# Two more pairs of tiles by seven products, the quarter sums of w_out in earlier slots, and batch 2 a slot sooner

## The chip, the core and the metric

One core of a Trainium2 chip runs the whole kernel. The metric is the device time of one execution in microseconds (us); where several executions are shown, it is their median. A profile is one execution, recorded by the hardware profiler. The engines are named as the profile names them: PE (matmul), PEld (PE's weight load), DVE (vector), ACT (scalar), POOL (GpSimd) and SP (sync, which only issues DMAs here).

## What is computed

Attention with a sliding window and a linear bias, then a two-layer network with ELU. q, k and v have 8 batches, 8 heads, 576 positions and a head size of 64; w_in is 512 x 2048, w_out 2048 x 512; everything is float32 in DRAM.

```
scores = q @ k.T / 8 ;  rel = i - j
scores = scores - slope[h] * |rel|   where 0 <= rel < 128, else -1e9
x = softmax(scores) @ v              # to 4608 tokens x 512 (batch, position; head, d)
h = x @ w_in
g = h if h > 0 else exp(h) - 1
out = g @ w_out                      # 4608 x 512
```

## The kernel before

All inputs are turned to float16 as they are loaded; sums are float32 in PSUM. The 4608 tokens are 9 blocks t of 512 (NTB = 9) for the second part, and 8 batches of 576 for the attention, so attention runs a little ahead of the blocks that use it.

**Slots.** The program's order is written out by hand (`tc.manual_schedule()`): each engine works through its instructions in the order in which the program gives them. A loop at the end (L655 on) goes through numbered slots s. In each slot it gives, in this order: the `early` entries; the hidden step of the slot (`HID`, one [128 x 512] PSUM bank of h: 16 or so matmuls of L305); `done(s-1)`, the DVE half of ELU for the slot before; the `tasks` (attention steps, turns, loads, sums); the output work of the slot (`OUT`); and the `late` entries. `at_once` puts an entry at the head of the tasks, `before` and `after` into `early` and `late`. Slots 0 to 17 hold the hidden steps of block 0 and two of block 1; slots 18 to 23 have no hidden step, as the first batch's positions are used up; from slot 24 on every slot has one. Slot 11 starts at about 34 us, slot 18 at 48.3, slot 24 at 57.2, slot 31 at 69.8, slot 38 at 84.6, slot 48 at 104.5.

**Hidden and ELU.** `hidden` (L297) computes h into one of two or three PSUM banks in turn (`BUF`), and ELU is max(min(exp(h), 1) - 1, h). In a plain slot ACT takes exp (L315), POOL clamps (L316); in a slot of the set `SOFT` ACT does both, as exp(-relu(-h)) in two instructions (L312, L313), and POOL does nothing. DVE then subtracts 1 and takes the maximum with the PSUM bank (L323, `elu`), into g, in the slot after. `e`, between ACT, POOL and DVE, is a ring of six tiles.

**Output.** A pair n is 256 tokens (two row tiles of 128; block t has pairs 2t and 2t+1). A pair is multiplied with w_out in one of two ways. The plain way (`output`, L327) takes 4 matmuls of 512 columns per slot, 32 for a pair; a tile's sum lies in one PSUM bank, is copied by ACT (`store`, L336) and sent by SP. The other way (Strassen's, in Winograd's form) takes the halves of the pair's rows, of the 2048 and of the 512, and needs seven products of quarter size (`product`, L387) instead of eight: 7 x 8 matmuls of 256 columns, seven matmuls to a slot over eight slots. For it DVE makes four sums of g per pair (`sums`, L363, 128 x 1024 float16 each), ACT keeps copies of four partial results (`kept`, L396) and copies one (L398), and DVE makes three combines (`combine`, L400: C11, C12, C22, 128 x 256 float32). Four sums of quarters of w_out, T[1] to T[4], are made once, by DVE, in eight halves (`quarters`, L356). The products of a pair accumulate in two PSUM banks, `XY[n]`: products 1, 6, 7 and 4 in the first, 2, 5 and 3 in the second; 6 has to wait until ACT has copied 1, 5 until C11 has read 2, and so on. `SEVEN` is the set of pairs done so.

**Attention.** From batch 2 on, `START[b]` is the slot in which a batch begins; unit u (128 keys against 256 queries) begins 4 slots after the one before. `scores` (L218) fills four banks (spa, sp[2], sp[3]), ACT takes exp in the next two slots (`expo`, L233 and L236), DVE multiplies with the bias table (`weigh`, L241), and three slots after the scores `all_values` (L263) multiplies with v into spa; DVE divides into `xn` (L277, L260), a ring of six tiles, and `turn` (L280) transposes it into xT, by DMA on SP from batch 2 on and on PE with a copy by ACT before. The last 64 rows of a batch (`values`, unit 4) use sp[2] and sp[3], one slot after unit 3. Batches 0 and 1 are done in smaller steps (`turn_first`, `first_scores`, `first_weigh`, `values`), batch 1 in slots 16 to 32, its q and k turned on PE (L136, copies L140).

The eight PSUM banks are spa (two), sp[2], sp[3], hp[0], hp[1], av and op.

Of the kernel before, what the change touches and what calls it, by code (L numbers as in the profile page):

```python
# [18 lines left out]
def kernel(  # L19
# [35 lines left out]
    RB = one([128, 512], F16, "RB")  # L55

    SI = one([128, H, 128], F16, "SI")
# [28 lines left out]

    T = [None] + [s1[:, 2048 * i:2048 * i + 2048].rearrange("p (j c) -> p j c", j=8) for i in range(3)]
    T.append(one([128, 8, 256], F16, "T4"))

# [59 lines left out]
    with tc.manual_schedule():  # L149
# [93 lines left out]
        def values(b, i, part, bank=av):  # L243

            m = 128 if i < 4 else 64
            banks = (part, part + 2) if b < 2 else (2 * part, 2 * part + 1)
            parts = [(3, 128, 3), (3, 192, 4)] if i == 4 else [(i, 0, i)] + ([(i - 1, 128, i - 1)] if i else [])
            a = bank[:, 0:4 * (D + 1)].rearrange("p (x h d) -> p x h d", x=2, h=2)
            for x, g in enumerate(banks):
                for h2 in range(2):  # L250
                    for j, (u, c, n) in enumerate(parts):
                        c += 512 * g + 256 * h2
                        nc.tensor.matmul(a[:, x, h2, :], ex_[u][:, c:c + 128], VP[b % 2][:, n, 2 * g + h2, 0:D + 1],  # L253
                                         start=j == 0, stop=j == len(parts) - 1)
            if part == 0:
                xnt[b, i] = work.tile([128, 4, 2, D], F16, name="xn", tag="xn", bufs=6)
            o = xnt[b, i][0:m, part::2, :, :] if b < 2 else xnt[b, i][0:m, 2 * part:2 * part + 2, :, :]
            r = work.tile([128, 2, 2], F32, name="rden", tag="rden", bufs=2)
            V.reciprocal(out=r[0:m], in_=a[0:m, :, :, D])
            V.tensor_tensor(out=o, in0=a[0:m, :, :, 0:D], in1=r[0:m].unsqueeze(3).broadcast_to([m, 2, 2, D]),  # L260
                            op=ALU.mult)

        def all_values(b, i):  # L263
# [9 lines left out]
            xnt[b, i] = work.tile([128, 4, 2, D], F16, name="xn", tag="xn", bufs=6)  # L273
# [23 lines left out]
        def hidden(t, c0, w, f0, nf, p, soft):  # L297
# [10 lines left out]
            e = es[t, c0, f0] = work.tile([128, 512], F32, name="e", tag="e", bufs=6)  # L308
# [111 lines left out]
        wz = one([128, 256], F16, "wz")  # L420
# [7 lines left out]
        rel = one([128, 256], I32, "rel")  # L428
        far = one([128, 256], F16, "far")
# [89 lines left out]
        SEVEN = range(3, 18)  # L519

        XY = {1: (op, av)}
        for n in range(2, 2 * NTB):
            XY[n] = XY[n - 1][::-1] if n - 1 in SEVEN else XY[n - 1]
        for o in range(16 * NTB):
# [4 lines left out]
            OUT[s] = [(output, (t, ts, 4 * f, (op, op, sp[3], op)[ts] if t == 0 else XY[o // 8 or 1][ts % 2]))]  # L529
# [52 lines left out]
        for u, a0, a1, d in ((0, 18, 19, 2), (1, 20, 21, 2), (2, 22, 24, 0), (3, 26, 28, 0)):  # L582
# [5 lines left out]
            at(a1 + 3, turn, 1, u, nc.scalar.copy, (op, av, sp[3], sp[3])[u])  # L588
        at(24, turn_first, 1, 1, 1, 0, sp[3], nc.scalar.copy)
# [5 lines left out]
        START = [None, None, 32, 48, 66, 83, 100, 117]  # L595
# [32 lines left out]
        for m, a in enumerate((26, 30, 31, 32, 34, 35, 36, 39)):  # L628
            at_once(a, quarters, 1 + m // 2, m % 2)
        turns = [(i, j) for i in (1, 2, 6, 5, 7, 3, 4) for j in range(8)]  # L630
        for n in SEVEN:
            s = 15 + 8 * n
            if n < 2 * NTB - 1:
                for d, i in ((-1, 1), (1, 2), (3, 3), (4, 4)):
                    at_once(s + d, sums, n, i)
                after(s + 2, combine, n, "C11")
                after(s + 6, combine, n, "C12")
                at_once(s + 8, combine, n, "C22")
                for d in range(8):
                    OUT[s + d] = [(product, (n, i, j, j + 1)) for i, j in turns[7 * d:7 * d + 7]]  # L640
# [10 lines left out]

        SOFT = {15 + 8 * n + d for n in SEVEN for d in (0, 1, 2, 3, 4, 7)} | {26, 30, 31, 32, 34, 35, 36, 39} | set(range(16 * NTB - 10, 16 * NTB + 8))

# [44 lines left out]
```

## Time and profile before

| | |
|---|---|
| Median of 5 runs | 313.14 us (312.75 to 313.47) |
| The profiled execution's own time | 312.75 us |
| Its span in the profile | 311.0 us |
| Busy: PE, weight loads | 301.9 us (97%), 251.6 us |
| Busy: DVE, ACT, POOL | 251.8 (81%), 238.0 (77%), 111.1 (36%) |
| L305 (hidden), PE | 1488 matmuls of L305 into hp, 144.3 us |
| L329 (plain output), PE | 96 matmuls in all |
| Granted PE clock | full speed in all slices |

The profile was recorded on one execution, whose own time lies 1.75 us over its span. A row of the view by stretches gives a window's start and end, its length, then for each engine the busy time and, in brackets, the number of instructions. A row of the timeline gives start and duration in us, engine and line, operation, what is written and what is read, the shapes and how many such instructions in a row; in square brackets stands the idle time before it and what ended it. A row of the chain of waits gives start, duration and line. Durations of neighbours on one engine may overlap a little, as engines take the next instruction before the last one's result is out; the distance from start to start is what an instruction holds its engine.

### The profile page before, as it was taken

What the parts mean: (1) busy time and instruction counts of PE and PEld (TensorE: products, weight loads), DVE (VectorE), ACT (ScalarE), POOL (GpSimd) and SP (SyncE); (2) the same over time, 40 slices, a digit from 0 to 9 for tenths busy, and PEclk for the clock granted to TensorE, in tenths of its full rate; (3) what the DMA queues carried; (4) which work ended last, traced back from release to release, by engine and by line L of the source; (5) the groups of instructions that cost most, each with busy time, mean ns of one, the idle gap of its engine ahead of it and who ended that gap; (6) DMA issues with size and microseconds to landing.
All of it is one profiled execution on the core that took longest, in us unless ns stands there. A gap on an engine that the chain in (4) does not pass through costs nothing.

```text
span 311.0 us, 9691 instructions
## 1 busy us (share of the span) xinstructions
PE 301.9 (97%) x4023; PEld 251.6 (81%) x4023; DVE 251.8 (81%) x484; ACT 238.0 (77%) x434; POOL 111.1 (36%) x169
## 2 busy tenths in 40 slices
PE   8799999999999999999999999999999999999995
PEld 6588774787678788988888888888899888888884
DVE  5646656789899999898989989989998788886783
ACT  5467448688878698888797889788888797968871
POOL 8748789462262316150707070806000101010000
PEclk9999999999999999999999999999999999999999
DMA  9999999987797919698999999999632312030103
GB/s 97 178 196 201 202 173 148 164 85 98 86 119 82 165 18 143 64 131 86 81 119 99 148 89 92 119 137 95 81 94 11 93 19 86 19 93 4 67 25 112
DMA packets 96508, 32.02 MB, mean 103 GB/s; under 512 B 83920, under 2 KB 91984, under 8 KB 96464
## 3 DMA queue, kind: packets, MB, share of 16 engines
q0 software_dynamic: 75920, 18.36, 66.0%
q1 hardware_dynamic: 20400, 12.98, 18.1%
q8 instruction: 31, 0.51, 0.7%
q14 instruction: 13, 0.11, 0.1%
q10 hardware_dynamic: 144, 0.07, 0.1%
HBM read 36.70 MB, written 9.44 MB: 148 GB/s over the span
## 4 chain that ended last, share of the span: by engine, by line
PE 80%; DVE 6%; DMA 4%; ACT 4%; POOL 4%; issue 2%; POOLq 0%; ACTq 0%
PE hp L305 35%; PE op L393 12%; PE av L393 12%; PE op L329 4%; PE spa L225 4%; DMA s<-in_q_dram 4%; PE spa L271 3%; DVE g L323 3%; POOL e L316 2%; ACT e L315 2%; PE sp L393 1%; PE sp L329 1%; PE sp L305 1%; PE sp L253 1%; PE av L329 1%
## 5 line engine op out<-in xcount | busy, mean ns | idle before, releaser
L305 PE MATMUL hp<-xT,wi 128*128 128x256 f16 (+3 forms) x1488 | 144.3, 245 | 1.8 <-DMA wi<-in_moe_w_in_dram 0.9
L305 PEld LDWEIGHTS <-wi 128*128 128x128 f16 x1600 | 119.4, 98 | 21.3 <-issue 6.7
L323 DVE SCALAR_TENSOR_TENSOR g<-e,hp 128x512 f16<-128x512 f32 x138 | 93.6, 679 | 26.7 <-POOL e L316 13.4
L316 POOL TENSOR_SCALAR e<-e 128x512 f32<-128x512 f32 x50 | 31.2, 625 | 159.8 <-ACT e L315 159.3
L312 ACT ACTIVATE e<-hp 128x512 f32<-128x512 f32 x94 | 56.3, 599 | 26.1 <-PE hp L305 22.2
L313 ACT ACTIVATE e<-e 128x512 f32<-128x512 f32 x94 | 59.4, 632 | 3.0
L393 PEld LDWEIGHTS <-S 128*128 128x128 f16 x480 | 45.6, 98 | 5.0
L315 ACT ACTIVATE e<-hp 128x512 f32<-128x512 f32 x44 | 26.5, 603 | 15.7 <-PE hp L305 14.4
L241 DVE TENSOR_TENSOR EX<-EX,TAB 128x1024 f16<-128x1024 f16 x48 | 33.4, 695 | 6.3 <-ACT EX L233 3.4
L393 PEld LDWEIGHTS <-g 128*128 128x128 f16 x360 | 33.9, 98 | 3.6
L114 POOL DMA_DIRECT2D VP<-in_v_dram x40 | 34.3, 866 | 2.3 <-DMA s<-in_q_dram 1.3
L233 ACT ACTIVATE EX<-spa 128x1024 f16<-128x1024 f32 x24 | 24.7, 1027 | 5.6 <-PE spa L225 5.3
L236 ACT ACTIVATE EX<-sp 128x512 f16<-128x512 f32 x48 | 26.0, 598 | 0.0
L393 PE MATMUL op<-s,S 128*128 128x256 f16 x168 | 25.2, 273 | 0.0
L393 PE MATMUL av<-s,S 128*128 128x256 f16 x168 | 25.2, 273 | 0.0
L354 DVE TENSOR_TENSOR S<-g 128x1024 f16<-128x1024 f16 (+2 forms) x31 | 20.8, 671 | 0.8 <-PE av L393 0.2
L277 DVE TENSOR_TENSOR xn<-spa,rden 128x512 f16<-128x512 f32 x24 | 16.6, 691 | 0.8
L393 PE MATMUL av<-wo,g 128*128 128x256 f16 x112 | 16.8, 272 | 0.0
L393 PE MATMUL op<-wo,g 128*128 128x256 f16 x112 | 16.8, 272 | 0.0
L329 PE MATMUL op<-wo,g 128*128 128x512 f16 x64 | 16.5, 379 | 0.0
L108 POOL DMA_DIRECT2D st<-in_k_dram x24 | 16.2, 682 | 0.1
L225 PE MATMUL sp<-QT,KT 32*128 32x256 f16 (+2 forms) x240 | 15.4, 250 | 0.7 <-DVE xn L260 0.7
(142 smaller groups left out, 388.3 us busy)
## 6 DMA issues: line engine op xcount, KB each, us to landing
out_dram<-ob SPq DMA_DIRECT2D x35, 256.0 KB, 2.6
VP<-in_v_dram POOLq DMA_DIRECT2D x32, 128.0 KB, 5.8
st<-in_k_dram POOLq DMA_DIRECT2D x24, 144.0 KB, 4.2
st<-in_q_dram POOLq DMA_DIRECT2D x24, 144.0 KB, 6.0
wi<-in_moe_w_in_dram POOLq DMA_DIRECT2D x4, 512.0 KB, 13.3
wo<-in_moe_w_out_dram POOLq DMA_DIRECT2D x4, 512.0 KB, 11.2
VP<-in_v_dram POOLq DMA_DIRECT2D x8, 64.0 KB, 5.9
s<-in_k_dram POOLq DMA_DIRECT2D x1, 512.0 KB, 13.1
```

The source lines that it names most:

```text
L114: nc.gpsimd.dma_start(VP[b % 2][0:p, n, :, 0:D], v[b, :, 128 * n:128 * n + p, :].rearrange("h p d -> p h d"))
L225: nc.tensor.matmul(sp[g][:, 256 * h2 + o:256 * h2 + o + n], kt_[b % 2][r, k0:k0 + 255:2], qt_[b % 2][r, c0:c0 + 2 * n - 1:2], start=dh == ...
L236: nc.scalar.activation(unit(b, u)[:, g, :, :], sp[g].rearrange("p (h c) -> p h c", h=2), AF.Exp, scale=0.125)
L241: V.tensor_tensor(out=e, in0=e, in1=TAB[:, int(u == 3), 2 * gp:2 * gp + 2, :, :], op=ALU.mult)
L305: nc.tensor.matmul(p[:, l * w + u0:l * w + u1], w_in_sb[:, c, fc * 128:(fc + 1) * 128], xT[:, c, x0:x0 + u1 - u0], start=(c == 0), stop=(c ...
L312: nc.scalar.activation(e[:, 0:n], p[:, 0:n], AF.Relu, scale=-1.0)
L313: nc.scalar.activation(e[:, 0:n], e[:, 0:n], AF.Exp, scale=-1.0)
L315: nc.scalar.activation(e[:, 0:n], p[:, 0:n], AF.Exp)
L316: nc.gpsimd.tensor_scalar(out=e[:, 0:n], in0=e[:, 0:n], scalar1=1.0, scalar2=0.0, op0=ALU.min, op1=ALU.max)
L323: V.scalar_tensor_tensor(out=gs[t][:, f0:f0 + nf, c0:c0 + w], in0=sh(es.pop((t, c0, f0))), scalar=1.0, in1=sh(hps.pop((t, c0, f0))), op0=A ...
L329: nc.tensor.matmul(o, gs[t][:, fc, ts * 128:(ts + 1) * 128], w_out_sb[:, fc, :], start=(fc == 0), stop=(fc == NFC - 1))
L393: nc.tensor.matmul(o, a[:, j, :], b[:, j, :], start=j == 0 and i in (1, 2, 5), stop=j == 7, skip_group_check=True)
```

## The change

- `SEVEN` grows from pairs 3 to 17 to pairs 1 to 17. Pair 0 alone stays plain. Pair 1 takes the slots that its plain form had, 19 to 23, 25, 27 and 29 (`ps`); pair 2 takes 31 to 38. The number of slots with output work is the same.
- The eight halves of T[1] to T[4] go from slots 26, 30 to 32, 34 to 36 and 39 to slots 11 to 18.
- T[1] to T[3] lay in `s1`, the staging tile of batch 1's q and k; they get tiles of their own. The room comes from `RB`, `SI`, `wz`, `rel` and `far`, small tables of the start, which now lie in those tiles, and from the rings of xn and e, four deep in place of six.
- `SOFT` becomes: slots 11 to 18, slots of pairs 2 to 17 by the old rule, and 20, 22 and 23 (which have no hidden step). So 11 to 17, 33 and 38 become soft, and 26, 30 and 36 plain.
- `START[2]` goes from 32 to 31: all of batch 2's attention is a slot sooner, and the loads for batch 3, which are placed by it, too. Batch 3 stays at 48.
- Banks: pair 1 uses op and sp[3]; from pair 2 on the two banks alternate; the turns of batch 1's units 0 and 2 use av, and the last turn of its k goes from slot 24 and sp[3] to slot 25 and av.

```diff
--- before.py
+++ after.py
@@ -52,9 +52,12 @@
     ident = one([128, 128], F16, "ident")
 
 
-    RB = one([128, 512], F16, "RB")
-
-    SI = one([128, H, 128], F16, "SI")
+
+    T = [None] + [one([128, 8, 256], F16, f"T{i}") for i in (1, 2, 3, 4)]
+    fore = [t.rearrange("p j c -> p (j c)") if t is not None else None for t in T]
+    RB = fore[3][:, 1024:1536]
+
+    SI = fore[3][:, 0:1024].rearrange("p (h c) -> p h c", h=H)
 
     TAB = one([128, 2, 4, 2, 256], F16, "TAB")
 
@@ -83,9 +86,6 @@
     s0 = gpool.tile([128, NFC * 512], F16, name="s0", tag="g")
     s1 = one([128, 2 * H * 6 * D], F16, "s1")
     s0 = [t[:, 0:2 * H * 6 * D].rearrange("p (w h j d) -> p w h j d", w=2, h=H, j=6) for t in (s0, s1)]
-
-    T = [None] + [s1[:, 2048 * i:2048 * i + 2048].rearrange("p (j c) -> p j c", j=8) for i in range(3)]
-    T.append(one([128, 8, 256], F16, "T4"))
 
     def split(b, w, part):
 
@@ -253,7 +253,7 @@
                         nc.tensor.matmul(a[:, x, h2, :], ex_[u][:, c:c + 128], VP[b % 2][:, n, 2 * g + h2, 0:D + 1],
                                          start=j == 0, stop=j == len(parts) - 1)
             if part == 0:
-                xnt[b, i] = work.tile([128, 4, 2, D], F16, name="xn", tag="xn", bufs=6)
+                xnt[b, i] = work.tile([128, 4, 2, D], F16, name="xn", tag="xn", bufs=4)
             o = xnt[b, i][0:m, part::2, :, :] if b < 2 else xnt[b, i][0:m, 2 * part:2 * part + 2, :, :]
             r = work.tile([128, 2, 2], F32, name="rden", tag="rden", bufs=2)
             V.reciprocal(out=r[0:m], in_=a[0:m, :, :, D])
@@ -270,7 +270,7 @@
                     c += 256 * h
                     nc.tensor.matmul(a[:, h // 4, h % 4, :], ex_[u][:, c:c + 128], VP[b % 2][:, n, h, 0:D + 1],
                                      start=j == 0, stop=j == len(parts) - 1)
-            xnt[b, i] = work.tile([128, 4, 2, D], F16, name="xn", tag="xn", bufs=6)
+            xnt[b, i] = work.tile([128, 4, 2, D], F16, name="xn", tag="xn", bufs=4)
             o = xnt[b, i][0:m].rearrange("p (t g) h d -> p t (g h) d", t=2)
             r = work.tile([128, 2, 4], F32, name="rden", tag="rden8", bufs=2)
             V.reciprocal(out=r[0:m], in_=a[0:m, :, :, D])
@@ -305,7 +305,7 @@
                         nc.tensor.matmul(
                             p[:, l * w + u0:l * w + u1], w_in_sb[:, c, fc * 128:(fc + 1) * 128],
                             xT[:, c, x0:x0 + u1 - u0], start=(c == 0), stop=(c == 3))
-            e = es[t, c0, f0] = work.tile([128, 512], F32, name="e", tag="e", bufs=6)
+            e = es[t, c0, f0] = work.tile([128, 512], F32, name="e", tag="e", bufs=4)
             n = w * nf
             if soft:
 
@@ -417,7 +417,7 @@
                 copy(tile_out(n, 1)[:, c0:c0 + 128], o[:, c0:c0 + 128])
                 put(n, 1, c0, c0 + 128, queue)
 
-        wz = one([128, 256], F16, "wz")
+        wz = fore[4][:, 0:256]
 
         def warm(n, bank=op):
             for _ in range(n):
@@ -425,8 +425,8 @@
 
 
 
-        rel = one([128, 256], I32, "rel")
-        far = one([128, 256], F16, "far")
+        rel = fore[3][:, 1536:2048].bitcast(I32)
+        far = fore[1][:, 0:256]
         V.memset(wz, 1.0)
         load_first(0, 1, 0)
         nc.gpsimd.iota(rel, pattern=[[1, 256]], base=0, channel_multiplier=-1)
@@ -516,17 +516,17 @@
             for j in range(16):
                 step = (256 * (j // 8), 256, 2 * (j % 8), 2)
                 HID[16 * t + 6 + j] = [(t, *step, BUF[(j + 1) % 2])]
-        SEVEN = range(3, 18)
-
-        XY = {1: (op, av)}
-        for n in range(2, 2 * NTB):
-            XY[n] = XY[n - 1][::-1] if n - 1 in SEVEN else XY[n - 1]
+        SEVEN = range(1, 18)
+
+        XY = {1: (op, sp[3]), 2: (op, av)}
+        for n in range(3, 2 * NTB):
+            XY[n] = XY[n - 1][::-1]
         for o in range(16 * NTB):
             t, ts, f = o // 16, o // 4 % 4, o % 4
             if o // 8 in SEVEN:
                 continue
             s = (9, 11, 13, 14)[o] if o < 4 else 11 + o if o < 13 else 2 * o - 1 if o < 16 else 15 + o
-            OUT[s] = [(output, (t, ts, 4 * f, (op, op, sp[3], op)[ts] if t == 0 else XY[o // 8 or 1][ts % 2]))]
+            OUT[s] = [(output, (t, ts, 4 * f, op))]
 
         def done(r):
             for step in HID[r]:
@@ -585,14 +585,14 @@
                 at(a, first_expo, 1, u, half, d * half, 0, 256)
                 at(a + 1, first_weigh, 1, u, half)
                 at(a + 2, values, 1, u, half, av if half else sp[2])
-            at(a1 + 3, turn, 1, u, nc.scalar.copy, (op, av, sp[3], sp[3])[u])
-        at(24, turn_first, 1, 1, 1, 0, sp[3], nc.scalar.copy)
+            at(a1 + 3, turn, 1, u, nc.scalar.copy, (av, av, av, sp[3])[u])
+        at(25, turn_first, 1, 1, 1, 0, av, nc.scalar.copy)
         at(30, values, 1, 4, 0, sp[2])
         at(31, values, 1, 4, 1)
         at(32, turn, 1, 4)
 
 
-        START = [None, None, 32, 48, 66, 83, 100, 117]
+        START = [None, None, 31, 48, 66, 83, 100, 117]
 
         TURN = [None, None, (22, 24, 25, 28), (40, 42, 44, 46)]
         REST = 32, 33, 36, 37
@@ -625,19 +625,20 @@
                 at(a + 3 + n if a else 20 + n // 2, load_v, b, n)
 
 
-        for m, a in enumerate((26, 30, 31, 32, 34, 35, 36, 39)):
+        for m, a in enumerate(range(11, 19)):
             at_once(a, quarters, 1 + m // 2, m % 2)
         turns = [(i, j) for i in (1, 2, 6, 5, 7, 3, 4) for j in range(8)]
         for n in SEVEN:
             s = 15 + 8 * n
+            ps = (19, 20, 21, 22, 23, 25, 27, 29, 30) if n == 1 else range(s, s + 9)
             if n < 2 * NTB - 1:
                 for d, i in ((-1, 1), (1, 2), (3, 3), (4, 4)):
-                    at_once(s + d, sums, n, i)
-                after(s + 2, combine, n, "C11")
-                after(s + 6, combine, n, "C12")
-                at_once(s + 8, combine, n, "C22")
+                    at_once(ps[d] if d > 0 else ps[0] - 1, sums, n, i)
+                after(ps[2], combine, n, "C11")
+                after(ps[6], combine, n, "C12")
+                at_once(ps[8], combine, n, "C22")
                 for d in range(8):
-                    OUT[s + d] = [(product, (n, i, j, j + 1)) for i, j in turns[7 * d:7 * d + 7]]
+                    OUT[ps[d]] = [(product, (n, i, j, j + 1)) for i, j in turns[7 * d:7 * d + 7]]
             else:
                 at_once(s - 3, sums, n, 3)
                 for i in (2, 1):
@@ -649,7 +650,7 @@
                               (product, (n, 4)), (last_out, (n,))]
 
 
-        SOFT = {15 + 8 * n + d for n in SEVEN for d in (0, 1, 2, 3, 4, 7)} | {26, 30, 31, 32, 34, 35, 36, 39} | set(range(16 * NTB - 10, 16 * NTB + 8))
+        SOFT = {15 + 8 * n + d for n in SEVEN[1:] for d in (0, 1, 2, 3, 4, 7)} | set(range(11, 19)) | {20, 22, 23} | set(range(16 * NTB - 10, 16 * NTB + 8))
 
         slots = set(HID) | set(OUT) | set(tasks) | set(early)
         for s in range(min(slots), max(slots) + 1):
```

## The prediction

> **What bounds the kernel now.** I read three views. First the busy time of each engine by stretch, cut at the slots that the change touches (35 to 50 us is slots 11 to 18, 50 to 60 slots 19 to 24, 60 to 75 slots 25 to 32, 88 to 108 slots 40 to 48):
>
> ```profile
> 35.00:50.00 15.00, 15.00 (x247) 10.59 (x243) 8.36 (x13) 8.23 (x13) 13.29 (x20) 1.00 1.61 165
> 50.00:60.00 10.00, 9.91 (x118) 5.77 (x115) 6.96 (x18) 7.45 (x13) 6.83 (x10) 1.00 1.82 171
> 60.00:75.00 15.00, 14.80 (x255) 11.37 (x253) 13.50 (x29) 11.33 (x20) 7.46 (x12) 1.00 0.99 117
> 88.00:108.00 20.00, 19.21 (x243) 15.94 (x242) 19.01 (x37) 15.56 (x29) 8.20 (x13) 1.00 1.11 131
> ```
>
> The columns after the length are PE, weight loads, DVE, ACT and POOL, then the granted clock. PE is full, at full clock: every matmul removed is time, unless PE then waits. DVE has 45% free in slots 11 to 18, 30% in 19 to 24, 10% in 25 to 32 and 5% in 40 to 48.
>
> Second, the chain of waits, for the pace of one slot's share of output work:
>
> ```profile
> 38.18 0.86 PE op L329 x4
> 87.98 0.76 PE op L393 x7
> ```
>
> A plain output step is 4 matmuls of 512 columns, 0.86 us (215 ns each); a product step is 7 of 256, 0.76 us (109 ns each).
>
> Third, the timeline by engine, for PE's few waits and for what ACT does in the slots that become soft:
>
> ```profile
> 90.32 0.28 PE L225 MATMUL spa<-QT,KT 32*128 32x256 f16 x2
> 90.89 1.05 PE L305 MATMUL hp<-xT,wi 128*128 128x256 f16 x8
> ...
> 106.77 0.29 PE L225 MATMUL spa<-QT,KT 32*128 32x256 f16 x2
> 107.46 0.27 PE L225 MATMUL sp<-QT,KT 32*128 32x256 f16 x1 [0.41 <-DVE xn L260]
> 107.99 0.27 PE L225 MATMUL sp<-QT,KT 32*128 32x256 f16 x1 [0.27 <-DVE xn L260]
> ...
> 108.54 1.05 PE L305 MATMUL hp<-xT,wi 128*128 128x256 f16 x8
> ```
> ```profile
> 40.83 0.59 ACT L336 COPY ob<-op 128x512 f32<-128x512 f32 x1 [0.27 <-PE op L329]
> ...
> 47.01 1.01 ACT L140 COPY QT<-hp 128x1024 f16<-128x1024 f16 x1
> ...
> 62.07 0.60 ACT L312 ACTIVATE e<-hp 128x512 f32<-128x512 f32 x1 [0.95 <-PE hp L305]
> 62.70 0.63 ACT L313 ACTIVATE e<-e 128x512 f32<-128x512 f32 x1
> 63.24 1.01 ACT L205 ACTIVATE EX<-spa 128x1024 f16<-128x1024 f32 x1
> ```
>
> Scores normally hold PE 0.57 us (90.32 to 90.89); in slot 48 they hold it 1.77, because batch 3's scores want sp[2] and sp[3] in the slot in which batch 2's last values are still being read out of them. And a soft ELU holds ACT 1.17 us (62.07 to 63.24), where the plain one holds it about 0.55.
>
> **What is gained.** (1) Pairs 1 and 2: 64 matmuls of 512 columns become 112 of 256, in the same 16 slots: 16 x (0.86 - 0.76) = -1.6 us of PE. No 256-column product runs slower elsewhere in this trace, so I take the whole. The Trainium skill ("TensorE: Matmul & The Clock Gate", Back-to-back issue gap) speaks against it: it gives a sustained spacing of 131 ns at 512 columns and 81 ns at 128. An estimate from that, about 98 ns at 256, would make a pair 56 x 98 = 5.5 us instead of 32 x 131 = 4.2, this term +2.6 and the whole sum below +2.9; this case's matmuls take 215 and 109 ns, not 131 and 98.
>
> (2) Batch 2 a slot sooner. Its last values fall into slot 47, so one hidden step and two output steps (2.4 us) lie between them and batch 3's scores, against about 1.4 us of DVE work (a combine, two reads). The wait of 1.77 - 0.57 = 1.2 us goes: -1.2. The same shift brings the DMA transpose for batch 2's first tile 2 us sooner; PE now waits 0.18 us for it ahead of slot 38 (four L329 from 83.55, the next L305 at 84.59: 1.04 against 0.86): -0.2.
>
> (3) The quarter sum of slot 26 (0.60 us of DVE) goes from in front of the read-out that the transpose of slot 27 waits for; that turn takes 0.44 us there (63.48 to 63.92) and 0.22 elsewhere: -0.2.
>
> The moved batch takes more with it: its five transposes on SP, each a slot sooner and ahead of a store that nobody waits for (SP issues ten DMAs in all between 73 and 108 us), and on POOL the loads for batch 3, which hang on batch 2's start; their buffers are read out by slot 31, and the loads of values come at 34 and later: nothing, or a little DMA traffic beside a transpose, which took from 2.9 us (issued 73.23) to 6.7 (issued 89.58, beside four loads). Slot 38 has 0.7 us to spare by my carrying.
>
> Gains: 3.2 us.
>
> **What is lost.** All engines take their queues in order, so I carried each queue by hand through slots 11 to 48 with the pitches of the rows: DVE 0.60 per elu, weigh, sum or quarter, 0.33 to 0.40 per combine, 0.56 per pair of reciprocal and read-out; ACT as above, 0.25 per kept copy. Where work stays hidden I say under what.
>
> (4) Slots 11 to 17 become soft: +0.6 us of ACT each, POOL's step gone. In slots of 1.75 us ACT has room, and the elus come no later (ACT 0.6 and POOL 0.6 before, ACT twice 0.6 after). But what stands behind the second ACT step in ACT's queue comes 0.6 later. Slot 14: the copy of op, now 40.83 to 41.42, would end at 41.74; slot 15's output, on op again, starts at 41.53 now, and would at 41.81: +0.28. Slot 17: the copy of QT, now 47.01 to 48.02, would end 0.6 later; the scores of slot 18, now at 48.32, wait for it: +0.38. Other copies behind soft steps have no reader for a slot or more. Bounds for the two together: 0, if ACT's pair fits ahead of them, and 1.2, two whole steps; I take the row sums, 0.66.
>
> (5) Slot 19's first product goes to op, not sp[3], while ACT is still copying slot 18's output out of op (the scores' exp is ahead of it): +0.23, between 0 and one whole copy, 0.59. The turn of slot 24 that goes to slot 25 and to av is the same work: nothing.
>
> (6) The eight quarters at 11 to 18: 0.60 us each under 1.75 us slots with 45% of DVE idle, behind the elu that PE needs. w_out's last quarter is issued at 26.05 and lands in about 12 us, before slot 14 (38.9): nothing. Without that cover they would cost 0.6 each.
>
> (7) Slots 18 to 23 have no hidden step and are short (1.3 to 1.7 us). DVE gets a last quarter, four sums and a combine there, 5 x 0.60 + 0.35 = 3.35 us against 3.4 us of DVE gaps between 48.6 and 60. Exp, weigh and values follow each other two slots apart, so order matters: sum 3 and the first combine stand ahead of the read-out and weigh that slot 23's values need. By hand weigh ends 0.66 us after PE wants it (0.21 now); slot 21's wait grows by 0.06: +0.5. Bounds: 0 (all in gaps) and 3.35. Behind it queue the products and, in ACT, the kept copies, which come in time.
>
> (8) Slot 30: the quarter ahead of the last read-out of batch 1 becomes a sum and a combine, 0.35 longer; slot 31's transpose on PE waits for it: +0.3 (0 if PE comes late anyway, 0.95 for both whole). The scores of batch 2 follow in slot 31 on sp[3], whose copy in ACT (behind a soft step) ends just as PE comes: 0, or up to +0.5 if late.
>
> (9) Slots 32 to 35: weighs, turns and sums of pair 2 now fall together, 7.4 us of DVE in 7.4 us of slots; the combine before product 5 and elu 33 come late by 0.17 each: +0.3. Slots 39 to 47: DVE has a quarter less and batch 2 shifted; one new wait of about 0.25 for the spa read-out, while two of about 0.2 (at 96.18 and 104.20) ease: -0.1. Bounds for all of (9): -0.4, the old waits gone and no new ones, and +1.1, one more wait of 0.25 to 0.3 in each of three steps.
>
> Losses: 0.28 + 0.38 + 0.23 + 0.5 + 0.3 + 0.3 - 0.1 = 1.9 us. The freed POOL issues its loads sooner; nobody waits for them. The smaller rings (e and xn, four deep) are not reached: a bank of hidden is rewritten after two or three slots and waits for the same elu.
>
> Sum: -3.2 + 1.9 = -1.3 us. The profiled execution took 312.75 (span 311.0), so 311.45 and a span of 309.7; the median of the runs lies 0.39 above it: 311.8.
>
> **The rivals.** A, slower: DVE becomes the bound of slots 18 to 24. All 3.35 us of (7) reach PE instead of 0.5: -1.3 + 2.85 = +1.5, 314.7. For it: DVE's gaps there are just as long as what is added, and PE idles there already for weighs. Against: gaps before reads of PE's own banks shrink when PE is late. It decides from about 1.8 us of the 3.35 on. B: slots 18 to 31 are paced by exp, weigh and values, so PE's 0.1 in each of pair 1's eight steps is only waited away: -1.3 + 0.8 = -0.5, 312.6. For it: PE waits for weighs in slots 21 and 23. C: the copies of (4) and (5) come in time, as ACT is only 55% busy there: -1.3 - 0.9 = -2.2, 310.9. Against: the order in ACT's queue. That the change does not do what it says is excluded: the built program has 48 more matmuls on PE and 14 more instructions on DVE, 2 x (56 - 32) and 2 x 7.
>
> **How the numbers follow.** Forecast 0.50, C 0.18, B 0.16, A 0.16. A measurement of this kernel tells about 0.2% (0.6 us) from no change. Faster: 0.47 of the forecast, all of C, 0.09 of B: 0.74. Same: 0.03, 0.06 and 0.03 of the forecast, B and A: 0.12. Slower: the rest, 0.14. The range reaches below C by a little and up to half of A, 310.3 to 313.4; a full A is left out.
>
> **What would show it.** Right: slot 48's scores take 0.57 us; the steps of slots 19 to 38 take 0.76; L393 gains 112 matmuls and L329 keeps 32; PE waits for ACT in slots 15, 18 and 19 and for DVE in 23 and 31. Wrong: a DVE without idle time from 49 to 60 us with PE waits of over 1.8 us there (A), no wait for ACT before slot 19 (C), or slots 19 to 24 as long as before (B).

## The result and the profile after

The changed kernel takes 311.96 us (median of 44 runs, 311.14 to 313.58), the kernel before 312.69 (85 runs, 311.21 to 316.77). The ratio is 0.9974 [0.9963, 0.9985]: 0.8 us faster, between 0.5 and 1.2. The forecast was 311.8 and "faster". The sign held, and 311.96 lies close to 311.8; but the step that was forecast, -1.3, is outside the interval. It was counted from 313.14, the median of five runs, and the median of 85 lies 0.45 below that. The terms held less well than the total: one was three times too small, another had the wrong sign, and a part of the difference lies where no term of mine was.

The busy time by stretch of the changed kernel (start and end, length, PE, weight loads, DVE, ACT, POOL, clock):

```profile
35.00:50.00 15.00, 14.62 (x237) 10.38 (x237) 12.79 (x21) 11.71 (x20) 10.67 (x16) 1.00 1.86 184
50.00:60.00 10.00, 9.28 (x124) 7.03 (x124) 8.78 (x22) 7.63 (x15) 5.10 (x8) 1.00 1.66 151
60.00:75.00 15.00, 13.93 (x272) 12.52 (x270) 13.33 (x29) 10.56 (x18) 10.78 (x15) 1.00 0.89 110
88.00:108.00 20.00, 19.50 (x258) 16.51 (x256) 18.70 (x36) 16.18 (x30) 7.26 (x11) 1.00 1.08 118
```

PE was full in the first three stretches and no longer is: 0.38, 0.72 and 1.07 us are idle where 0, 0.09 and 0.20 were. DVE went from 8.36 to 12.79 and from 6.96 to 8.78 in the first two. The clock is 1.00 throughout. PE's work became less, as meant, and a good part of it came back as waits.

PE's rows where the prediction had its terms, in the changed kernel's timeline (the bracket is the idle time ahead of the row and who ended it):

```profile
48.37 0.40 PE L176 MATMUL spa<-QT,KT 64*128 64x256 f16 x4 [0.27 <-ACT QT L140]
...
56.51 0.41 PE L253 MATMUL av<-VP,EX 128*128 128x65 f16 x8 [0.47 <-ACT U L396]
...
71.81 0.34 PE L289 MATMUL sp<-ident,xn 128*128 128x128 f16 x3 [0.92 <-DVE xn L260]
...
97.70 1.03 PE L305 MATMUL hp<-xT,wi 128*128 128x256 f16 x8 [0.33 <-DVE g L323]
...
105.55 1.03 PE L305 MATMUL hp<-xT,wi 128*128 128x256 f16 x8 [0.17 <-DVE g L323]
...
107.28 0.29 PE L225 MATMUL spa<-QT,KT 32*128 32x256 f16 x2
...
107.84 1.05 PE L305 MATMUL hp<-xT,wi 128*128 128x256 f16 x8
```

The last two rows are the gain: slot 48's scores hold PE from 107.28 to 107.84, 0.56 us instead of 1.77. The largest loss is the third, slot 31, where the transposes of batch 1's last values wait 0.92 us for DVE's read-out. In the kernel before, all four of them stand in one row without such a wait:

```profile
70.72 0.61 PE L289 MATMUL sp<-ident,xn 128*128 128x128 f16 x4
```

The chain of waits of the changed kernel shows that the product step kept its price: seven matmuls in 0.76 us, 109 ns each.

```profile
72.39 0.76 PE op L393 x7
```

ACT's rows for the two soft slots of term (4):

```profile
40.63 0.57 ACT L336 COPY ob<-op 128x512 f32<-128x512 f32 x1
...
46.79 0.63 ACT L313 ACTIVATE e<-e 128x512 f32<-128x512 f32 x1
47.33 0.99 ACT L140 COPY QT<-hp 128x1024 f16<-128x1024 f16 x1
```

Both copies now stand behind the soft pair: the one of op ends at 41.20 where the output step on op began at 41.25, and the one of QT ends at 48.32, 0.05 before the scores of slot 18.

**Stage by stage.** The distance between the first hidden matmuls of two slots, from the trace, in us; the two kernels were profiled three and two times in all (second and third profiles are the runs at the end of the experiments):

```
slots       before                    after
            1st    2nd    3rd         1st    2nd
up to 0     13.37  13.42  13.83       13.51  13.99
0 to 11     20.54  20.66  19.83       19.84  19.83
11 to 49    74.63  74.63  74.90       74.50  74.49
  15 to 16   1.76   1.76   1.76        2.03   2.03
  17 to 24  11.88  11.88  11.88       12.50  12.50
  27 to 28   2.20   2.20   2.20        1.89   1.89
  31 to 32   2.44   2.44   2.44        3.87   3.88
  37 to 38   1.94   1.77   2.35        1.66   1.66
  48 to 49   3.98   3.99   4.00        2.30   2.30
49 to 149   190.41 190.32 190.42      190.55 190.49
```

Within a kernel the rows repeat to 0.02 us unless a DMA decides them (up to 0, 0 to 11, 37 to 38, and small parts of 49 to 149; up to 0 counts from the first instruction). In the region that the change edits, the change is worth only -0.13 us against two of the three profiles of before, -0.4 against the third.

### The profile page after: what moved, and what is told of

Read it like the earlier page. It is cut to its first block, busy times and chain, and to the rows that moved or that the text cites. A ratio compares the mean times of both kernels' runs of the same rounds, so it can differ in the third digit from the quotient of the medians.

```text
span 310.5 us, 9820 instructions
## 1 busy us (share of the span) xinstructions
PE 299.5 (96%) x4071; PEld 256.3 (83%) x4071; DVE 258.6 (83%) x498; ACT 242.3 (78%) x446; POOL 108.9 (35%) x163
## 4 chain that ended last, share of the span: by engine, by line
PE 77%; DVE 8%; ACT 7%; issue 3%; DMA 2%; POOL 2%; POOLq 0%; ACTq 0%; DVEq 0%
PE hp L305 34%; PE op L393 13%; PE av L393 13%; PE spa L225 4%; DVE g L323 3%; PE spa L271 3%; PE sp L393 2%; DMA s<-in_q_dram 2%; ACT EX L236 2%; PE op L329 1%; POOL e L316 1%; PE sp L305 1%; ACT e L315 1%; PE sp L253 1%; ACT e L312 1%
## 5 line engine op out<-in xcount | busy, mean ns | idle before, releaser
L323 DVE SCALAR_TENSOR_TENSOR g<-e,hp 128x512 f16<-128x512 f32 x138 | 93.7, 679 | 23.0 <-ACT e L313 12.9
L316 POOL TENSOR_SCALAR e<-e 128x512 f32<-128x512 f32 x44 | 28.1, 639 | 158.1 <-ACT e L315 153.0
L313 ACT ACTIVATE e<-e 128x512 f32<-128x512 f32 x100 | 63.2, 632 | 3.2
L393 PEld LDWEIGHTS <-S 128*128 128x128 f16 x544 | 51.4, 98 | 6.0 <-issue 0.5
L393 PEld LDWEIGHTS <-g 128*128 128x128 f16 x408 | 38.2, 98 | 4.7 <-issue 0.6
L393 PE MATMUL op<-T,S 128*128 128x256 f16 x200 | 30.0, 273 | 0.0
L393 PE MATMUL av<-T,S 128*128 128x256 f16 x176 | 26.4, 272 | 0.1
L354 DVE TENSOR_TENSOR S<-g 128x1024 f16<-128x1024 f16 (+2 forms) x35 | 23.5, 673 | 0.8 <-PE op L393 0.2
L393 PE MATMUL op<-wo,g 128*128 128x256 f16 x128 | 19.2, 272 | 0.1
L108 POOL DMA_DIRECT2D st<-in_q_dram x24 | 15.9, 671 | 0.9 <-DMA VP<-in_v_dram 0.9
L271 PE MATMUL spa<-VP,EX 128*128 128x65 f16 x336 | 15.3, 194 | 0.1
```

The lines of the kernel that those rows point to most:

```text
L108: nc.gpsimd.dma_start(st[b][32 * g:32 * g + 32, w, :, :, :, :].rearrange("p h n j d -> p (h n) (j d)"), (q, k)[w][b, 2 * g:2 * g + 2, :, : ...
L271: nc.tensor.matmul(a[:, h // 4, h % 4, :], ex_[u][:, c:c + 128], VP[b % 2][:, n, h, 0:D + 1], start=j == 0, stop=j == len(parts) - 1)
L313: nc.scalar.activation(e[:, 0:n], e[:, 0:n], AF.Exp, scale=-1.0)
L316: nc.gpsimd.tensor_scalar(out=e[:, 0:n], in0=e[:, 0:n], scalar1=1.0, scalar2=0.0, op0=ALU.min, op1=ALU.max)
L323: V.scalar_tensor_tensor(out=gs[t][:, f0:f0 + nf, c0:c0 + w], in0=sh(es.pop((t, c0, f0))), scalar=1.0, in1=sh(hps.pop((t, c0, f0))), op0=A ...
L393: nc.tensor.matmul(o, a[:, j, :], b[:, j, :], start=j == 0 and i in (1, 2, 5), stop=j == 7, skip_group_check=True)
```

## The experiments

Stage times, the sum of slots 11 to 49 above all, are exact to about 0.02 us where no DMA decides, much sharper than the run times. The ratios are of run times, against the kernel before.

```
                 11 to 49   17 to 24   31 to 32   48 to 49   49 to 149   ratio, 95% interval
before            74.63      11.88       2.44       3.98      190.41
after             74.50      12.50       3.87       2.30      190.55     0.9974 [0.9963, 0.9985]
quarters_only     75.22      12.21       2.22       3.99      191.29     1.0015 [0.9993, 1.0038]
no_pair1          73.94      12.22       3.42       2.30      190.50     0.9936 [0.9910, 0.9961]
after_start32     75.98      12.50       3.21       3.34      190.47     1.0005 [0.9979, 1.0030]
before_start31    75.24      11.88       3.42       2.30      192.21     1.0041 [1.0017, 1.0065]
plain11           75.07      13.38       3.88       2.30      190.45     0.9995 [0.9978, 1.0012]
soft30            74.10      12.50       3.46       2.29      190.73     0.9985 [0.9964, 1.0005]
c22_late          74.00      12.49       3.42       2.29      190.46     0.9972 [0.9942, 1.0001]
tuned             73.19      12.23       3.42       2.30      190.50     0.9930 [0.9903, 0.9956]
tuned2            72.54      12.24       2.78       2.30      190.44     0.9888 [0.9858, 0.9917]
```

**quarters_only** is the changed kernel without its new products and without the shift, so the quarters in slots 11 to 18 and the soft slots alone (the lines that give pairs 1 and 2 their old banks are left out here).

```diff
-        SEVEN = range(1, 18)
+        SEVEN = range(3, 18)        # XY and the output banks as before
...
-        START = [None, None, 31, 48, 66, 83, 100, 117]
+        START = [None, None, 32, 48, 66, 83, 100, 117]
```

> The kernel after with pairs 1 and 2 back in the plain form and batch 2 back at slot 32: only the early quarter sums, their tiles and the soft slots 11 to 17 are left of the change. Measured from the first hidden matmul of slot 11 to that of slot 49 the kernel before takes 74.64 us and the kernel after 74.49. Theory (waits add up as in the prediction): +0.6 for ACT's copies in slots 15 and 18, -0.2 and -0.25 for the turns of slots 27 and 31 that no longer stand behind a quarter sum: 74.8, that is +0.15. Rival (the early quarters are free, ACT's waits are hidden elsewhere): 74.2, 0.45 less than before.

Slots 11 to 49 took 75.22. The waits of slots 15 and 18 are there to the hundredth (15 to 16: 2.03; 17 to 24: +0.33), the quarters themselves cost nothing, and slots 27 to 28 gave back 0.21, 31 to 32 0.22. But 37 to 38 took 2.41 (PE waited 0.48 there for a DMA transpose of batch 2, issued at 79.73 and landed at 84.11), which is about what 75.22 lies over the theory's 74.8, and another came late in slot 61, where PE's row is

```profile
134.13 1.03 PE L305 MATMUL hp<-xT,wi 128*128 128x256 f16 x8 [0.87 <-DMA xT<-xn]
```

So the preparation alone is no gain (ratio 1.0015, its interval contains 1); it only makes room.

**no_pair1** leaves pair 1 plain, on its old banks, and keeps all else.

```diff
-        SEVEN = range(1, 18)
+        SEVEN = range(2, 18)        # XY and the output banks as before
```

> The kernel after with pair 1 back in the plain form. Theory: PE takes 0.8 us more for the matmuls, but the waits of slot 19 (0.18), the added wait of slot 23 (0.33) and the longer DVE queue ahead of slot 31's transpose (a combine that held DVE 0.76) go: slot 11 to 49 in 74.49 + 0.8 - 0.18 - 0.33 - 0.76 = 74.0, faster than after by 0.5. Rival (pair 1 brings its 0.8 and the waits move elsewhere): 75.0 to 75.3, slower than after by 0.5 to 0.8.

73.94, as the theory had it, and the ratio is 0.9936: better than the whole change. Pair 1 by seven products costs 0.56 us of stage time, where my own terms for it (-0.8, and 0.23, 0.5 and 0.3 of losses) came to +0.2. Its PE time is not missing: the rows of slots 19 to 23 are shorter by 0.1 each. There they are waited away, ahead of the product of slot 19 and of the values of slots 21 and 23, whose waits fall back in no_pair1 to those of before: 17 to 24 takes 12.50 us with the products and 12.22 without. In slots 25, 27 and 29 the 0.1 each is kept (24 to 31: 12.25 against 12.45, with 0.1 more in slot 30), and slot 31 costs 0.45 (3.87 against 3.42).

**after_start32** and **before_start31** put the shift of batch 2 to the test, once taken out of the changed kernel and once put alone into the kernel before.

```diff
-        START = [None, None, 31, 48, 66, 83, 100, 117]
+        START = [None, None, 32, 48, 66, 83, 100, 117]
```

> The kernel after with batch 2 back at slot 32. Theory: the wait of batch 3's scores in slot 48 is back (+1.2) and the one for the DMA transpose ahead of slot 38 (+0.2), while the waits of slots 34 and 35 (0.4) and 45 to 48 (0.3) ease: 74.49 + 0.7 = 75.2. Rival (the earlier start only moves the DVE load, and the gain of slot 48 is paid in slots 31 to 47): 74.5, no difference.

> The kernel before with batch 2 at slot 31 and nothing else changed. Theory: -1.2 in slot 48, -0.2 ahead of slot 38, and about +0.3 in slot 31, where the scores now come while ACT still copies sp[3] behind a soft step: 74.64 - 1.1 = 73.5, about 0.35% faster than before and faster than the whole change. Rival (DVE's weighs, turns and quarters fall together in slots 32 to 35 and cost as much): 74.3 to 74.6.

Without the shift the changed kernel needs 75.98 in 11 to 49, 1.48 more: in this region the gain is the shift's. Slots 48 to 49 took 3.34 (2.30 with the shift), and the hidden step of slot 46 waited 1.50 us for an ELU of DVE (L323), which neither theory had: the total is 0.8 beyond the theory's 75.2.

Alone in the kernel before, the shift fails: 75.24, where the theory had 73.5 and the rival at most 74.6, and the ratio is 1.0041. Slots 48 to 49 take 2.30 as in the changed kernel, so that mechanism is right; but slots 31 to 34 took 6.94 instead of 6.63, and in slot 38 PE stood

```profile
86.57 1.03 PE L305 MATMUL hp<-xT,wi 128*128 128x256 f16 x8 [1.39 <-DMA xT<-xn]
```

for a transpose issued at 80.27 and landed at 86.43. Three of POOL's loads of values were issued just ahead of it, at 78.03, 78.95 and 79.82. In the changed kernel the same transpose is issued at 80.78 and lands at 83.18, 2.4 us: no load is issued between 72.46 and 84.12. The DMAs of that stretch in before_start31 (issues, kilobytes each, median us to landing):

```profile
VP<-in_v_dram POOLq DMA_DIRECT2D x4, 128.0 KB, 4.6
...
xT<-xn SPq DMA_TRANSPOSE x1, 6.2
```

POOL has one queue for clamps and loads, so which slots are soft decides when loads go out: in before_start31 the clamp of slot 33, at 77.45, stands ahead of the loads of 78.03; in the changed kernel slots 31 to 35 are soft, no clamp comes between 69.87 and 83.56, and two of these loads went out at 71.57 and 72.46. That the loads make the transpose late is read from such pairs of rows; no run moved the loads alone. In slot 61 the same kernel lost another 1.8 us (61 to 62: 3.48 instead of 1.7). The profiled execution was the longest of its twelve (315.47, median 314.33), so not every run lost this much.

**plain11** keeps the change and makes slots 11 to 18 plain.

```diff
-        SOFT = {...} | set(range(11, 19)) | {20, 22, 23} | ...
+        SOFT = {...} | {20, 22, 23} | ...
```

> The kernel after with slots 11 to 18 plain again: the clamp of ELU back on POOL there, while DVE makes the quarter sums. Slots 11 to 17 take PE 23.9 us before (from 11 to 24, 23.28) and 24.18 after. Theory: the waits of slots 15 (0.28) and 18 (0.33) go, as nothing holds the copies in ACT's queue: slot 11 to 49 in 74.50 - 0.6 = 73.9. Rival (the soft slots are needed: clamp and quarter sum slow each other as the combine and the clamp of slot 30 did, and elus come too late for PE): 74.5 or more, with PE waiting for DVE in L305 of slots 13 to 18.

My theory fell. Slot 15's wait went, as it should (1.76), but 17 to 24 rose to 13.38 and the sum to 75.07. PE waits there for DVE, most of all for a weigh in slot 20, and not in the hidden steps of slots 13 to 18, where the rival had looked:

```profile
50.81 0.30 PE L253 MATMUL sp<-VP,EX 128*128 128x65 f16 x4 [0.54 <-DVE EX L216]
```

DVE's rows show no idle time from 42.95 to 52.50, so what one of them loses is passed on to the weighs. The loss is in these rows of DVE and POOL:

```profile
45.89 1.32 DVE L354 TENSOR_TENSOR T<-wo,T 128x1024 f16<-128x1024 f16 x1
```
```profile
43.61 1.10 POOL L316 TENSOR_SCALAR e<-e 128x512 f32<-128x512 f32 x1
...
46.04 0.62 POOL L316 TENSOR_SCALAR e<-e 128x512 f32<-128x512 f32 x1
```

A quarter takes 0.68 alone and a clamp 0.61 alone. The quarter of 43.56 kept its 0.68 and the clamp of 43.61 took 1.10; the quarter of 45.89 took 1.32 and the clamp beside it kept its 0.62. One of the two waits for the other. The soft slots thus do work that I had not seen: they keep POOL's clamps away from the quarters.

**soft30** makes slot 30 soft again, as it was before, with the same reason in mind.

```diff
-        SOFT = {...} | {20, 22, 23} | ...
+        SOFT = {...} | {20, 22, 23, 30} | ...
```

> The kernel after with slot 30 soft. In the kernel after, the combine of two SBUF tiles in slot 30 took 0.83 us beside a clamp on POOL that took 1.06. Theory (DVE and POOL slow each other there): without the clamp the combine takes about 0.41 as elsewhere, and PE's wait in slot 31 falls from 1.09 by 0.4: slot 11 to 49 in 74.1. Rival (the wait is only the length of DVE's queue): combine and wait as in the kernel after, 74.5.

This settles slot 31. In the changed kernel slot 30 is plain, and DVE and POOL meet:

```profile
69.76 0.69 DVE L354 TENSOR_TENSOR S<-g 128x1024 f16<-128x1024 f16 x1
70.37 0.83 DVE L354 TENSOR_TENSOR ob<-U,U 128x256 f32<-128x256 f32 x1
```
```profile
69.87 1.06 POOL L316 TENSOR_SCALAR e<-e 128x512 f32<-128x512 f32 x1 [0.23 <-ACT e L315]
```

The sum runs at its own pace to 70.45, the clamp, begun inside it, ends at 70.93, half a microsecond after the sum; and the combine, begun at 70.37, ends at 71.20. In soft30, without the clamp:

```profile
69.35 0.42 DVE L354 TENSOR_TENSOR ob<-U,U 128x256 f32<-128x256 f32 x1
```
```profile
70.37 0.34 PE L289 MATMUL sp<-ident,xn 128*128 128x128 f16 x3 [0.51 <-DVE xn L260]
```

0.42 instead of 0.83, and PE's wait falls from 0.92 to 0.51: the same 0.41. The trace of the changed kernel also holds the counterpart. A C12, at 101.38 us, has one operand in PSUM (op), lies beside a clamp for its whole length, and neither is slowed. It is one of eleven such combines beside a clamp in this trace, and all took 0.38 to 0.42:

```profile
101.38 0.41 DVE L354 TENSOR_TENSOR ob<-U,op 128x256 f32<-128x256 f32 x1
```
```profile
101.33 0.61 POOL L316 TENSOR_SCALAR e<-e 128x512 f32<-128x512 f32 x1 [0.55 <-ACT e L315]
```

The Trainium skill has this rule ("SBUF — State Buffer", Who interferes with whom): a DVE instruction with two inputs in SBUF contends with a GpSimd instruction that reads SBUF, the lock on the ports that the two share is exclusive, and a DVE instruction with at most one such input does not contend, outside modes that use both ports. These rows agree: sum and combine with two SBUF operands contend with the clamp, the later one ends 0.4 to 0.6 us late where the other still had about 0.6 to run, and the combine with a PSUM operand doesn't. In plain11 the quarter's row begins 0.15 us ahead of the clamp that it waits for, but inside the row of DVE's step before it (45.30 to 45.98), so the start of a row is not quite the moment that decides.

**c22_late** moves C22 of pair 1 behind the read-outs, two slots later.

```diff
-                at_once(ps[8], combine, n, "C22")
+                (at if n == 1 else at_once)(ps[8] + 2 * (n == 1), combine, n, "C22")
```

> The kernel after with pair 1's last combine moved from the head of slot 30 to the end of slot 32's tasks. Theory: it leaves the queue ahead of the read-out that slot 31's transpose waits for, which comes 0.76 sooner: slot 11 to 49 in 74.50 - 0.76 + 0.1 for its new place = 73.8. Rival (DVE is as full in slot 32, so that the waits of slots 34 and 35 grow by as much): 74.5.

74.00: the wait for the read-out falls from 0.92 to 0.17, 0.75 us, but 31 to 32 only from 3.87 to 3.42. no_pair1, before_start31 and tuned stop at the same 3.42, whatever was eased on DVE (soft30 at 3.46). There is a second floor, and the profile of tuned names it.

**tuned** puts together what the others suggested: slots 14, 17 and 18 plain (the waits of term (4)), C22 of pair 1 one slot later, the sums (2, 1) and (1, 3) behind the attention steps of their slots, and DVE's turns of q and k for batches 2 and 3 (`REST`, `TURN[3]`) moved to other slots.

```diff
-        TURN = [None, None, (22, 24, 25, 28), (40, 42, 44, 46)]
-        REST = 32, 33, 36, 37
+        TURN = [None, None, (22, 24, 25, 28), (39, 43, 44, 45)]
+        REST = 32, 35, 36, 37
...
-                    at_once(ps[d] if d > 0 else ps[0] - 1, sums, n, i)
+                    (at if (n, i) in ((2, 1), (1, 3)) else at_once)(ps[d] if d > 0 else ps[0] - 1, sums, n, i)
...
-                at_once(ps[8], combine, n, "C22")
+                (at if n == 1 else at_once)(ps[8] + (n == 1), combine, n, "C22")
...
-        SOFT = {...} | set(range(11, 19)) | {20, 22, 23} | ...
+        SOFT = {...} | {11, 12, 13, 15, 16} | {20, 22, 23} | ...
```

> The kernel after with five DVE steps and two ELUs in other places: slots 14 and 17 plain; pair 1's sum 3 and pair 2's sum 1 at the end of their slots' tasks; pair 1's last combine at the end of slot 31; batch 2's second turn of k from slot 33 to 35; batch 3's turns from 40, 42, 44, 46 to 39, 43, 44, 45. Theory (the change's losses are places in queues): waits of slots 15, 18, 23, 31, 34, 35 and 45 to 48 shrink by 0.6 + 0.3 + 0.8 + 0.3 + 0.3: slot 11 to 49 in 72.2, about 0.7% faster than the kernel after. Rival (DVE is simply full from slot 18 to 47, and a wait that is taken away appears at the next step): 73.7 or more.

73.19, between theory and rival; ratio 0.9930. PE in slot 31 of tuned:

```profile
72.27 0.27 PE L225 MATMUL sp<-QT,KT 32*128 32x256 f16 x1 [0.37 <-ACT xT L290]
```

and ACT ahead of it:

```profile
70.49 0.60 ACT L312 ACTIVATE e<-hp 128x512 f32<-128x512 f32 x1 [1.09 <-PE hp L305]
71.11 0.63 ACT L313 ACTIVATE e<-e 128x512 f32<-128x512 f32 x1
71.65 0.57 ACT L290 COPY xT<-sp 128x512 f16<-128x512 f16 x1
```

Batch 2's scores want sp[3], and its copy stands behind the soft pair of slot 31. Term (8) had named this copy as "0, or up to +0.5 if late", and I had taken 0.

**tuned2** makes slot 31 plain.

```diff
+        SOFT -= {31}
```

> The tuned kernel with slot 31 plain again (its ELU's second ACT step and clamp on ACT become ACT once and POOL). Theory: in the tuned kernel the scores of slot 31 wait 0.37 us for ACT's copy of sp[3], which stands behind the soft pair of slot 31 (0.60 + 0.63 us of ACT); with one ACT step of 0.6 less in front of it that wait goes, the stretch of slots 31 to 32 falls from 3.42 to 2.7 us or less, slots 11 to 49 from 73.19 to about 72.5, a ratio to the kernel before of about 0.991. Rival: POOL's clamp of slot 31 now runs beside DVE's read-outs and sums, both take longer (as 0.41 to 0.83 and 0.61 to 1.06 in slot 30 of the changed kernel), and DVE gives it back: slots 11 to 49 at 73.2 or above, ratio 0.993.

```profile
70.26 0.58 ACT L290 COPY xT<-sp 128x512 f16<-128x512 f16 x1
```
```profile
70.89 0.29 PE L225 MATMUL spa<-QT,KT 32*128 32x256 f16 x2
```

The copy of sp[3] now begins at 70.26 and ends at 70.84, before the scores; 31 to 32 falls to 2.78 and slots 11 to 49 to 72.54, 2.0 us under the changed kernel. The ratio is 0.9888 (309.80 us, median of 6, against 313.43, 11 runs): 1.1% under the kernel before, and the fastest of all. POOL's clamp meets no two-operand step of DVE there.

**before_again, before_again2, after_again** are the two kernels unedited, for more profiles of them.

> The kernel before once more, nothing edited, for a second profile of it. Theory: its slots 11 to 49 repeat (74.63 us within 0.1) and its start to slot 11 is about 19.8, as with all the others, so that the 0.5 us by which the profiled spans differ is chance of one execution's first loads; and where the runs differ by more, it is a wait for a DMA transpose (ahead of slot 38 or in slots 61 and 62, 0.5 to 2 us) that comes in some executions. Rival: the start is 20.5 again, so the change itself shortens the start; 49 to 149 as before (190.4).

> The kernel before a third time, nothing edited. Theory and rival as for the second: start 19.8 against 20.5, slots 11 to 49 at 74.63 within 0.1 unless a DMA transpose comes late, slots 49 to 149 at 190.4 or, with such a wait, 0.5 to 2 us more.

> The changed kernel once more, nothing edited, for a second profile of it. Theory: slots 11 to 49 repeat (74.50 us within 0.1), slot 31 to 32 is 3.87 again (it is set by engines, not by a DMA), start 19.8; 49 to 149 at 190.5. Rival: the 0.87 us wait in slot 31 is chance of one execution and is 0.3 here, as forecast.

The table of stages above has them. Slot 31's 3.87 repeats (3.88), so its wait is no chance. Of the start, my theory (chance) and the rival (the change shortens it) each have a case. From slot 0 to 11 before took 20.54, 20.66 and 19.83, the changed kernel 19.84 and 19.83, and before_start31, whose start is that of the kernel before, 19.66. In the longer ones PE waits for a first load instead of for DVE, here in the first profile of before:

```profile
15.54 0.44 PE L136 MATMUL sp<-ident,s 64*64 64x64 f16 x16 [0.88 <-DMA s<-in_q_dram]
```

So by these slots the longer start is not bound to the old code, but came in two of its three profiles and in none of the ten of the changed kernel and its edits (19.48 to 19.84).

The stretch up to slot 0 belongs to the start as well, and with it the rival has the better case. From the first instruction to slot 11 the three profiles of before took 33.66 to 34.08 us and before_start31 34.19 (its PE clock was at half from 8.5 to 11.9 us, which no other of these profiles shows in its start); the ten took 32.33 to 33.82, and only after_again, the 33.82, reaches into the range of before; on each of the two chips that ran both starts the order is the same but for it. The third load of q is issued between 7.04 and 7.25 us in all fourteen; it landed at 16.92 to 18.80 in the four with the old start and at 15.55 to 17.70 in the ten. What makes the loads land sooner no run shows: the change does not touch their order, only where tables and tiles lie.

## Why the prediction held, and where it did not

Point by point, against waits read as the distance from start to start less the usual one:

- **(1) -1.6, product steps.** The price holds (0.76). The worth does not: by no_pair1 pair 1 costs 0.56 us, though its products were to save 0.8. That is not rival B, who let the 0.8 be waited away on top of all losses: in slots 25, 27 and 29 it arrives, and in 17 to 24 the forecast's own terms for products, copies and weighs (-0.5 + 0.38 + 0.23 + 0.5 = +0.61) are what was measured, 12.50 - 11.88 = +0.62. Pair 1 was a loss of 0.2 by the forecast's terms already, and slots 30 and 31 made it larger. The estimate from the matmul spacing of the Trainium skill ("TensorE: Matmul & The Clock Gate", Back-to-back issue gap), 2.9 us slower, is far off: 256 columns cost 109 ns here.
- **(2) -1.2 and -0.2.** Slot 48: 1.77 to 0.56, -1.21. Slot 38's wait is gone (37 to 38: 1.66 against 1.77 to 2.35, of which 0.1 is the product step). What I missed is that this rests on POOL: "the freed POOL issues its loads sooner; nobody waits for them" is wrong by the rows of before_start31: the transposes come late behind loads issued just ahead of them.
- **(3) -0.2.** 27 to 28: -0.31, of which 0.1 is the product.
- **(4) +0.28 and +0.38.** +0.27 and +0.33, by the row sums. Rival C is out.
- **(5) +0.23.** +0.18.
- **(6) 0.** Right, though under a condition that I had not written: the slots have to be soft (plain11).
- **(7) +0.5.** Slot 23's wait grew by 0.43 and slot 21's by 0.10: +0.53. (The row of slot 23 names ACT's copy into U, which ended at 56.50; the weigh that I had named ended at 56.45, so either fits.) Rival A, all 3.35 us of it, did not come; DVE had idle time and PE's was 0.72 us there (49 to 60 us), not over 1.8.
- **(8) +0.3.** The step that was mis-sized: +0.87. I priced the combine alone, at 0.33 to 0.40 from rows in which nothing lay beside it or an operand was in PSUM, and did not ask what becoming plain does to slot 30: +0.41 to 0.43 for combine against clamp, shown by soft30. The rest of the 0.87 is the combine's own 0.33 and 0.11 at the sum: it reads the g that elu writes and begins 0.72 us after elu does (0.73 in soft30), where the quarter in its place began 0.61 after. Under this wait lies the one for the copy of sp[3], which shows once the first is gone: 3.42 to 2.78 in tuned2.
- **(9) +0.3 and -0.1.** Slots 34 and 35: 0.42. Slots 39 to 47: of the old waits of 0.20 and 0.24 one stayed at 0.12, and the other returned as 0.33 in slot 48, with a new one of 0.33 in slot 44: +0.34 where I had -0.1. tuned moved its turns and sums for these and has 2.31 and 2.16 in 43 to 44 and 47 to 48 where the changed kernel has 2.70 and 2.45 (43 to 48 in all: 10.11 against 10.54).

Added up, -1.6 - 1.21 - 0.2 - 0.2 = -3.2 and 0.27 + 0.33 + 0.18 + 0.53 + 0.87 + 0.42 + 0.34 = +2.94: -0.3 us, where slots 11 to 49 show -0.13. The gains were all in their slots; the losses were 1.0 larger than forecast, 0.6 of it in (8) and 0.4 in the second part of (9). So by its own steps the forecast should have come out near 312.8 and not at 311.8. That 311.96 was measured all the same is luck: half of the 0.9 between is the five-run median from which the forecast counted, and the other half lies where it had no term.

That the runs still differ by 0.8 us has another place, most likely the start: up to slot 11 the profiles of before took 33.66 to 34.08 us and those of the changed kernel 33.35 and 33.82. Slot 37 adds a little (37 to 38: 1.77 to 2.35 in before, 1.66 in both profiles of after). The same holds for the edits of the changed kernel, whose ratios lie 0.3 to 1.5 us below what slots 11 to 149 say: tuned2 gains 2.1 us by these slots and 3.5 by the ratio, and in its profile the way to slot 11 is 1.4 us shorter than in the first of before.

A small part is the clock. The record gives each run's mean granted PE clock for 71 runs of before (those beside the experiments) and 45 of the changed kernel. With 0.998 or more the medians are 312.49 (57 runs, up to 314.57) and 311.90 (40 runs, up to 312.56); with 0.995 or less 313.69 (14 runs) and 313.34 (5 runs). So among runs of equal clock 0.6 us of the difference stays. No profile of a run of before beyond 313 us was taken, so the cause of its long runs stays open, and no step of mine had forecast this part.

## What to carry to other kernels

Price a moved vector step with what runs beside it after the move, and by where its operands lie: beside a clamp on POOL a combine of two SBUF operands took 0.83 us instead of 0.42 here, and one with an operand in PSUM kept its 0.41. Where a wait is removed, look for the next one under it before counting the gain (slot 31 had two), and take work off the matmul engine only where that engine, and not the exp-weigh-values chain, sets the pace. Moving a step on a queue moves the transfers behind it as well; a DMA transpose that is just in time should be read together with the loads issued ahead of it.

## What the runs showed that was not expected

- DVE and POOL hold each other up over most of an instruction: 0.41 to 0.83 (combine of two SBUF operands), 0.68 to 1.32 (quarter), 0.61 to 1.06 and 1.10 (clamp), and no loss in eleven combines with one operand in PSUM.
- DMA transposes took from 2.4 to 8.2 us from issue to landing within a single execution of the changed kernel (after_again).
